# Order of the first chunks in a spectral-mixing + SwiGLU kernel: narrow rows from PSUM, split second layer, SyncE's queue reordered

## Chip, cores, metric

The kernel runs on one core of a Trainium2 chip. The metric is device time in microseconds (us) of one launch. A core has TensorE (PE, matrix products into PSUM), VectorE (DVE), ScalarE (ACT), GpSimd (POOL) and SyncE (SP), which here only issues DMAs. Each engine works through its own instructions in the order in which the program gives them, and waits where an operand isn't there or where a buffer is still in use. SP's and POOL's DMA issues are such instructions too: one that waits holds up everything behind it in its queue.

## What is computed

The input x is 4096 x 640 in fp32. The block is a layer norm with scale and shift from a condition vector (`h = LN(x)*(1+ca)+sa`), a Fourier mixer, a gated residual, a second modulated layer norm, a SwiGLU and a second gated residual:

```python
Xf = rfft2(h);  z = Xf.reshape(..., NB=4, BS=160)          # 4 blocks of 160 columns
hr = relu(zr@w1[0] - zi@w1[1] + b1[0]);  hi = relu(zi@w1[0] + zr@w1[1] + b1[1])     # layer 1
or_ = hr@w2[0] - hi@w2[1] + b2[0];       oi_ = hi@w2[0] + hr@w2[1] + b2[1]          # layer 2
Yf = softshrink(or_ + 1j*oi_, 0.01);     x = x + ga * irfft2(Yf)
x = x + gb * ((silu(h2@w_gate) * (h2@w_up)) @ w_down)      # h2: second modulated layer norm of x
```

Products are made to fp32 accuracy from a rounded upper part and a lower part (fp32r) of each factor: upper x upper, lower x upper, upper x lower. So each weight and each activation has an "upper" instruction (round) and a "lower" one (value minus upper).

## The kernel before

The transform over 4096 positions is split as 128 x 32. **Stage a** (dft_a, dft_c) transforms the eight tiles xa0 to xa7 (each 128 x 4 x 640) over the first index and writes them to DRAM with write_s1(t, f): f = 0 and f = 1 are a quarter of the rows each (320 KB per tile), f = 2 is the other half (640 KB per tile). The rows written with f = 0 feed chunks 0 and 1, those with f = 1 chunks 2 and 3, those with f = 2 chunks 4 to 7. load_g(ch) reads a chunk back in the other layout into g (1,280 KB, two buffers), so chunk 2 needs every f = 1 write landed, and chunk 2's buffer is chunk 0's.

**Per chunk** (eight chunks, blocks b = 0 to 3 of 160 columns = 128 wide + 32 narrow):
- stage_b(ch, t) (matmuls of L612): second transform of 128 columns into a PSUM bank pb; t = 0 to 3 are the wide columns of the blocks, t = 4 the four blocks' narrow 32 columns together. Its banks are single buffers "b0" (t < 4) and "b1" (t = 4); (0,1) and (0,3) use the pair "p2" instead.
- evac_b (L619 on ACT, L620 on DVE): upper and lower part of the wide columns, z.
- the narrow rows rz, all four blocks of which layer 1 needs as 128 partitions. For chunk 0, evac_r(0, b) makes them from PSUM, 2 ACT instructions (L642) and 2 DVE instructions (L652) of 32 partitions for each block. For chunks 1 to 7, rem_high (L662) and rem_low (L666) evacuate all of pb into rt, rem_move (L675) writes rt to DRAM, and rem_read (L681) reads it back in four DMAs with the partitions regrouped. For chunk 1 both go by POOL's queue, for the others by SP's.
- stage_l1(ch, b) (21 matmuls of L707): two 128-wide outputs in the PSUM pair "p1" and a third, narrow one in "p3"; ACT rounds with relu (L724, L725), DVE makes the lower part (L726); tail_l1 (L743, L744) the narrow rest r2.
- stage_l2(ch, b) (16 matmuls of L764, two groups q of eight, in the PSUM pair "p2"); DVE adds the bias b2t and writes tt (L766).
- later: move_x (L780, SP: tt regrouped into xx), shrink, the inverse transform stage_i and a write to s2 by POOL.

The loop over p = 4 ch + b (L879) interleaves these over chunks: at p it does stage_l1(p), the next chunk's stage_b, stage_l2(p - 1). For p = 0 (L885 to L895) all four stage_l1 of chunk 0 come first, then the six lower parts of layer 2's weights (weights_low, L286, on DVE); p = 1 to 3 then do stage_b(1, ...) and stage_l2(0, 0 to 2); p = 4 starts with stage_l1(1, 0).

**Weights of layer 2**: six jobs prep2 in the order w2a, w2a, w2b, w2b, w2c, w2c; each an upper part (weights_high, L281 on POOL) and a lower part (weights_low, L286 on DVE), 128 x 640.

**Memory that is reused.** The pool p2 (right side) takes over the memory of xa0 to xa7 tile by tile, each tile waiting only for the users of what lay there. Both pools end at the same edge; per partition xp has 8 x 10,240 = 81,920 bytes and p2 78,336, so p2 begins 3,584 bytes further in. Its tiles lie in the order of first use: acc, cl, wx, bx (6,656 bytes), w2a, w2b, w2c (10,240 each), tt (2 x 5,120), wm, xx, xh, xl, co.

**SP's queue** (L489 to L547): half of chunk 0's load, the weights w2 (L252, L253), write_s1 of tiles 2 and 3, load_g(1) (L310), b2t (L514), a 16-element copy s1h out of g1 (L515), so that SP waits there until g1 has landed, then write_s1 of tiles 0, 4, 5, 6, 7 for f = 1 and again for f = 2, load_g(2), small constants (idn, tx, bx) and the first of the mod_load (L547).

Of the kernel before, what the change touches and what calls it, by code (L numbers as in the profile page):

```python
# [171 lines left out]
def body(tc, x, w1, b1, w2, b2, wg, wu, wd, c, wm, k_fa, k_tb, k_tx, k_bm, k_bx, k_ga, k_ge, k_id, out, dbg=None):  # L172
# [10 lines left out]
    s2 = nc.dram_tensor("s2", (128, N2, D), F32, kind="Internal").ap()  # L183
    s1h = nc.dram_tensor("s1h", (1, 16), F32, kind="Internal").ap()
    rzd = nc.dram_tensor("rzd", (NCH, 128, 4, 258), F32, kind="Internal").ap()
# [16 lines left out]
    with ExitStack() as top:  # L202
# [34 lines left out]
        with ExitStack() as af:  # L237
# [95 lines left out]
            with tc.tile_pool(name="sp", bufs=1) as sp:  # L333
# [157 lines left out]
                for job in jobs[6:]:  # L491
                    weights_high(*job)
                write_s1(7, 0, rest)
                load_g(0, 16, 32, None, rest)
                raws[2] = load_weights(rp, w2, "2")
                for t in (2, 3):
                    for f in (1, 2):
                        write_s1(t, f)

# [9 lines left out]

            hp = af.enter_context(tc.tile_pool(name="hp", bufs=1, reuse_waits="tile"))  # L510
            load_g(1)
            load_tb(1)
            b2t = hp.tile([P, 2, NB, BS], F32, name="b2t")
            nc.sync.dma_start(b2t, b2.rearrange("r b o -> (r b o)").partition_broadcast(P))  # L514
            nc.sync.dma_start(s1h, gs[1][127:128, 3, 0:16])  # L515
            for f in (1, 2):
                for t in (0, 4, 5, 6, 7):
                    write_s1(t, f)
            load_g(2)
            load_tb(2)  # L520
            stx.close()

# [12 lines left out]
            prep2 = [prep2[k] for k in (0, 3, 1, 4, 2, 5)]  # L535
            for job in prep2:
                weights_high(*job, pool)
# [68 lines left out]
            def stage_b(ch, t):  # L606
                g, tb = gs[ch], tbs[ch]
                pb = (ps.tile([P, 2, 256], F32, tag="p2", name=f"pb{ch}_{t}") if (ch, t) in ((0, 1), (0, 3)) else
                      bank0(1 if t == 4 else 0, [P, 2, 256], f"pb{ch}_{t}"))
                col = slice(128 * t, 128 * t + 128)  # L610
                for j in range(4):
                    mm(pb[:, :, 64 * j:64 * j + 64], g[:, j, col], tb[:, j, :], start=True, stop=True)  # L612
                pbs[ch, t] = pb
# [59 lines left out]
            def rem_move(ch):  # L673
                NN = width(ch)
                (pool if ch == 1 else nc.sync).dma_start(rzd[ch, :, :, 0:NN], f32(rts[ch].rearrange("p l i k -> p (l i) k")[:, :, 0:NN]))  # L675

            def rem_read(ch):
                NN = width(ch)
                r = rzs[ch] = hp.tile([P, NB, 258], F32R, tag="rz", bufs=2, name=f"rz{ch}")
                for q in range(4):  # L680
                    (pool if ch == 1 else nc.sync).dma_start(f32(r[32 * q:32 * q + 32, :, 0:NN]),  # L681
                                      rzd[ch].rearrange("(b e) q k -> q e b k", b=NB)[q, :, :, 0:NN])

            def stage_l1(ch, b):
                NN = width(ch)
                z = zs[ch, b]
                r = rzs[ch][:, b, :]
                hs = []
                pls, seqs = [], []
                for o in range(2):  # L690
                    pls.append(ps.tile([P, 512], F32, tag="p1", name=f"pl{ch}_{b}_{o}"))
                    cs = slice(128 * o, 128 * o + 128)
                    cl = slice(256 + 128 * o, 384 + 128 * o)
                    seqs.append([(w1a[:, b, cs], z[:, 0, 0, :NN]), (w1a[:, b, cs], z[:, 1, 0, :NN]),
                                 (w1a[:, b, cl], z[:, 0, 0, :NN]),
                                 (w1b[:, b, cs], z[:, 0, 1, :NN]), (w1b[:, b, cs], z[:, 1, 1, :NN]),
                                 (w1b[:, b, cl], z[:, 0, 1, :NN]),
                                 (w1c[:, b, cs], r[:, :NN]), (w1c[:, b, cl], r[:, :NN])])
# [20 lines left out]
                for o in range(2):  # L719
# [5 lines left out]
                    act.activation(h[:, 0, :NN], pl[:, :NN], AF.Relu, bias=b1m[:, o, b:b + 1])  # L725
                    dve.tensor_tensor(h[:, 1, :NN], h32[:, :NN], f32(h[:, 0, :NN]), op=OP.subtract)  # L726
                    hs.append(h)
                if not early:
# [6 lines left out]
                act.activation(u0[:, :NN], pl[64:128, :NN], AF.Copy)  # L735
                dve.scalar_tensor_tensor(u1[:, :NN], pl[0:64, :NN], b1r[:, b:b + 1], u0[:, :NN],
                                         op0=OP.add, op1=OP.add)
                hss[ch, b] = (hs[0], hs[1], r2, u1)
# [9 lines left out]
            def stage_l2(ch, b, then=()):  # L748
                h0, h1, r2, _ = hss[ch, b]
                de = slice(160 * b, 160 * b + 160)  # L750
                for q in range(3 if ch == CE else 2):
# [3 lines left out]
                    if b == 0 and q < 2:  # L755
# [5 lines left out]
                           (h1[:, 0, fs], w2b[:, b, 320:320 + W]),  # L761
                           (r2[:, fs], w2c[:, b, 0:W]), (r2[:, fs], w2c[:, b, 320:320 + W])]
                    for i, (l, m) in enumerate(seq):
                        mm(pc[:M, :W], l, m, start=(i == 0), stop=(i == len(seq) - 1))  # L764
                    if q < 2:
                        dve.tensor_tensor(tts[ch, q][:, :, de], pc[:, :320].rearrange("p (r e) -> p r e", r=2),  # L766
                                          b2t[:, :, b, :], op=OP.add)
                        if then:
                            then[q]()
                    else:  # L770

                        dve.tensor_tensor(tts[ch, 0][0:1, 1, de], pc[0:1, :160], b2t[0:1, 0, b, :], op=OP.add)

            xxs = {}
# [102 lines left out]
            cf = []  # L877

            for p in range(LAST + 1):  # L879
                ch, b = p // 4, p % 4  # L880
                on(shrink, p - 6)
                if p > 3:
                    on(stage_l1, p)

                if p == 0:  # L885
                    for q in range(4):
                        stage_l1(0, q)
                        for t in ((1, 2), (3,), (), ())[q]:
                            stage_b(0, t)
                            evac_b(0, t)  # L890
                            evac_r(0, t)
                        tail_l1(0, q)
                    for job in prep2:
                        weights_low(*job)
                    continue  # L895
                elif b == 0:
                    todo = [(ch, 3)]
# [3 lines left out]
                for q in todo:  # L901
                    stage_b(*q)
                    if q[1] < 4:
                        evac_b(*q)
                for f, *a in sums.get(p, ()):
                    f(*a)
                if b == 1 and ch + 1 < NCH:
                    rem_high(ch + 1)
                if p > 3:
                    on(tail_l1, p)  # L910
                on(shrink_high, p - 6)
# [1567 lines left out]
```

## Time and profile before

| | us |
|---|---|
| median of 3 runs (lowest, highest) | 1466.19 (1465.18, 1467.83) |
| profiled execution: device time | 1462.63 |
| profiled execution: span, first to last instruction | 1460.8 |
| TensorE busy in the span | 1408.0 (96%) |
| mean granted TensorE clock | 0.994 |

The profile is of one execution. In it an instruction's row gives its start, its duration, the engine, the line, output <- inputs and, in brackets, how long the engine sat idle before it and what released it. "SPq" is an issue by SP. A row of the windows gives, for each engine, busy time and number of instructions, then the granted TensorE clock (1.00 is full), the busy share of the DMA engines and what they moved.

### The profile page before, as it was taken

How to read it: one execution, taken by the hardware profiler on the slowest of the kernel's cores; microseconds unless marked ns; L12 is line 12 of the kernel's file. 1: busy time of each engine (PE TensorE's matmuls, PEld its weight loads, DVE VectorE, ACT ScalarE, POOL GpSimd, SP SyncE). 2: the span in 40 equal slices, each digit the busy share in tenths (PEclk: the TensorE clock that was granted, in tenths of full speed). 3: DMA queues.
4: the chain of work that ended last, by engine and by line, in shares of the span. 5: the costliest groups of instructions: out<-in, count | busy, mean ns of one | idle time of the engine just before them, and what ended most of it. 6: DMA issues, size and time to landing. Idle time of an engine off the chain costs nothing.

```text
span 1460.8 us, 23921 instructions
## 1 busy us (share of the span) xinstructions
PE 1408.0 (96%) x8516; PEld 1331.2 (91%) x8516; DVE 1081.5 (74%) x1967; ACT 782.2 (54%) x1550; POOL 551.3 (38%) x647
## 2 busy tenths in 40 slices
PE   6969999998999999999999999999999999999998
PEld 2669999966888888899999999999999999999998
DVE  8848877878787797757787868787747767567775
ACT  7828888744545455544565546555435445245432
POOL 5300100044555354322445424444324545146533
PEclk9989999999999999999999999999999999999999
DMA  9877767748677998798977997877696666966552
GB/s 378 313 230 225 241 190 228 221 144 271 240 276 261 334 310 267 272 370 290 311 263 244 343 368 256 312 247 253 229 344 219 228 209 239 357 207 238 204 183 88
DMA packets 186473, 380.05 MB, mean 260 GB/s; under 512 B 22226, under 2 KB 104082, under 8 KB 184562
## 3 DMA queue, kind: packets, MB, share of 16 engines
q1 hardware_dynamic: 177826, 361.09, 71.9%
q0 software_dynamic: 6944, 14.82, 3.3%
q10 hardware_dynamic: 1584, 2.62, 0.5%
q8 instruction: 67, 1.10, 0.3%
q14 instruction: 52, 0.43, 0.1%
HBM read 263.91 MB, written 105.39 MB: 253 GB/s over the span
## 4 chain that ended last, share of the span: by engine, by line
PE 59%; DVE 8%; DMA 6%; issue 2%; ACT 2%; POOL 1%; SPq 0%; POOLq 0%; ACTq 0%; DVEq 0%
PE pd L2347 12%; PE pw L2026 7%; PE pw L2028 7%; PE pw L2027 7%; PE pd_X L2207 4%; DMA cr<-s 3%; PE pg L1890 2%; PE pg L1891 2%; PE pd_Y L2207 2%; PE pg L1892 2%; PE pw L2037 2%; PE pw L2038 2%; PE pw L2039 2%; DVE wb L1344 2%; PE pd_Z L2207 1%
## 5 line engine op out<-in xcount | busy, mean ns | idle before, releaser
L2347 PE MATMUL pd<-wdh,a 128*128 128x320 f32 x1040 | 238.9, 310 | 1.0 <-DVE a L1927 0.6
L2347 PEld LDWEIGHTS pd<-wdh,a 128*128 128x128 f32 x1040 | 176.2, 188 | 2.0 <-DVE a L1927 0.9
L1344 DVE TENSOR_TENSOR wb<-r,wb 128x512 fp32r<-128x512 f32 (+3 forms) x156 | 159.5, 1030 | 17.2 <-ACT wb L1341 14.6
L2347 PE MATMUL pd<-wdl,a 128*128 128x320 f32 x540 | 166.2, 309 | 0.0
L2026 PE MATMUL pw<-h,wt 128*128 128x384 f32 x416 | 140.9, 339 | 2.3 <-ACT s_x L2045 1.2
L2028 PE MATMUL pw<-h,wt 128*128 128x384 f32 x416 | 140.4, 337 | 0.0
L2027 PE MATMUL pw<-h,wt 128*128 128x384 f32 x416 | 139.8, 336 | 0.0
L1341 ACT ACTIVATE wb<-r 128x512 fp32r<-128x512 f32 (+3 forms) x172 | 117.9, 703 | 34.0 <-PE pw L2039 24.6
L2319 DVE TENSOR_TENSOR x<-x,pd 128x320 f32<-128x320 f32 x240 | 108.9, 477 | 36.4 <-PE pd L2347 32.6
L2028 PE MATMUL pw<-h,wb 128*128 128x384 f32 x312 | 105.1, 337 | 2.3 <-DVE wb L1344 2.3
L2026 PE MATMUL pw<-h,wb 128*128 128x384 f32 x312 | 105.4, 338 | 0.0
L2027 PE MATMUL pw<-h,wb 128*128 128x384 f32 x312 | 105.0, 336 | 0.0
L1890 PE MATMUL pg<-ht,wb 128*128 128x512 f32 x260 | 103.0, 396 | 1.5 <-ACT wb L1341 1.5
L1892 PE MATMUL pg<-ht,wb 128*128 128x512 f32 x260 | 101.7, 391 | 2.2 <-DVE wb L1344 2.2
L2347 PEld LDWEIGHTS pd<-wdl,a 128*128 128x128 f32 x540 | 101.4, 188 | 0.5
L1891 PE MATMUL pg<-ht,wb 128*128 128x512 f32 x260 | 101.4, 390 | 0.0
L2045 ACT ACTIVATE s_x<-pw 128x384 f32<-128x384 f32 x52 | 25.5, 490 | 114.3 <-PE pw L2028 113.6
L1603 POOL TENSOR_TENSOR cr<-cr,gab 128x640 f32<-128x640 f32 x28 | 47.4, 1694 | 103.2 <-DMA cr<-s 83.2
L2026 PEld LDWEIGHTS pw<-h,wt 128*128 128x128 f32 x416 | 78.3, 188 | 4.2 <-ACT s_x L2045 2.2
L821 POOL DMA_DIRECT2D s<-co x28 | 15.8, 564 | 168.2 <-ACT co L820 160.5
L2027 PEld LDWEIGHTS pw<-h,wt 128*128 128x128 f32 x416 | 78.3, 188 | 0.0
L2028 PEld LDWEIGHTS pw<-h,wt 128*128 128x128 f32 x416 | 78.3, 188 | 0.0
(335 smaller groups left out, 4054.3 us busy)
## 6 DMA issues: line engine op xcount, KB each, us to landing
wt<-td SPq DMA_DIRECT2D x104, 512.0 KB, 5.3
hs<-ho SPq DMA_DIRECT2D x52, 512.0 KB, 5.0
h<-hs SPq DMA_DIRECT2D x32, 768.0 KB, 8.4
r<-in_B_w_gate_dram SPq DMA_DIRECT2D x36, 640.0 KB, 4.9
r<-in_B_w_up_dram SPq DMA_DIRECT2D x36, 640.0 KB, 5.3
wdr<-wdd SPq DMA_DIRECT2D x21, 640.0 KB, 4.9
td<-wt SPq DMA_DIRECT2D x25, 512.0 KB, 5.4
g<-s SPq DMA_DIRECT2D x7, 1280.0 KB, 9.3
```

Of the source, the lines that this page charges most:

```text
L1341: act.activation(wbs[t, n][:, 0, ks, e], raw[t, n][:, ks, e], AF.Copy)
L1344: (pool if onp else dve).tensor_tensor(wbs[t, n][:, 1, ks, e], raw[t, n][:, ks, e], f32(wbs[t, n][:, 0, ks, e]), op=OP.subtract)
L1603: pool.tensor_tensor(crs[r], crs[r], gab, op=OP.mult)
L1890: mm(b, wh, hh, start=(kk == 0), stop=False)
L1891: mm(b, wh, hl, start=False, stop=False)
L1892: mm(b, wl, hh, start=False, stop=(kk == 4))
L2026: mm(b, w(0, kp), a[:, kp, 0], start=start and kp == 0, stop=False, skip_group_check=not start)
L2027: mm(b, w(0, kp), a[:, kp, 1], start=False, stop=False, skip_group_check=not start)
L2028: mm(b, w(1, kp), a[:, kp, 0], start=False, stop=kp == 1, skip_group_check=not start)
L2207: mm(bk[b, i][:, :320], x, y, start=new and j == 0, stop=j == len(seq) - 1, skip_group_check=not new)
L2319: dve.tensor_tensor(x2[:, e], x2[:, e], x[0][:, :320], op=OP.add)
L2347: mm(pd[g, hf][0][:, :320], l, m, start=i == 0, stop=i == len(s) - 1 and not (last and len(gs) > 1))
```

## The change

Four things are done. (1) Chunk 1's narrow rows are made from PSUM by evac_r, as chunk 0's are, and its rem_high, rem_low, rem_move and rem_read fall away. (2) The first blocks get an order of their own, first_blocks(): layer 2's lower parts come earlier (two after stage_l1(0, 1), four before stage_l1(0, 2)), the two upper parts of w2c go from POOL to ACT, stage_l1(0, 2)'s three DVE instructions are put off, stage_l2(0, 0) and (0, 1) come before stage_l1(0, 3), and stage_l2(0, 0) does all products that need no lower weight first, for both q, and the three others of each at the end. (3) stage_b(0, 3) uses "b0" instead of "p2". (4) On SP, the f = 1 writes of tiles 2 and 3 come ahead of chunk 0's last load, tile 4's writes and b2t ahead of load_g(1), the copy s1h is gone, and load_g(2) comes ahead of the f = 2 writes of tiles 6, 7 and 0.

```diff
                 write_s1(7, 0, rest)
+                for t in (2, 3):
+                    write_s1(t, 1)
                 load_g(0, 16, 32, None, rest)
                 raws[2] = load_weights(rp, w2, "2")
-                for t in (2, 3):
-                    for f in (1, 2):
-                        write_s1(t, f)
+                for t, f in ((2, 2), (3, 2), (4, 1), (4, 2)):
+                    write_s1(t, f)
...
+            b2t = hp.tile([P, 2, NB, BS], F32, name="b2t")
+            nc.sync.dma_start(b2t, b2.rearrange("r b o -> (r b o)").partition_broadcast(P))
             load_g(1)
             load_tb(1)
-            b2t = hp.tile([P, 2, NB, BS], F32, name="b2t")
-            nc.sync.dma_start(b2t, b2.rearrange("r b o -> (r b o)").partition_broadcast(P))
-            nc.sync.dma_start(s1h, gs[1][127:128, 3, 0:16])
-            for f in (1, 2):
-                for t in (0, 4, 5, 6, 7):
-                    write_s1(t, f)
+            for t in (5, 0, 6, 7):
+                write_s1(t, 1)
+            write_s1(5, 2)
             load_g(2)
             load_tb(2)
+            for t in (6, 7, 0):
+                write_s1(t, 2)
             stx.close()
...
-            for job in prep2:
+            for job in prep2[:4]:
                 weights_high(*job, pool)
...
-                pb = (ps.tile(..., tag="p2", ...) if (ch, t) in ((0, 1), (0, 3)) else
+                pb = (ps.tile(..., tag="p2", ...) if (ch, t) == (0, 1) else
                       bank0(1 if t == 4 else 0, [P, 2, 256], f"pb{ch}_{t}"))
...
-            def stage_l1(ch, b):
+            def stage_l1(ch, b, later=None):
...
-                    dve.tensor_tensor(h[:, 1, :NN], h32[:, :NN], f32(h[:, 0, :NN]), op=OP.subtract)
+                    lows.append(lambda h=h, h32=h32: dve.tensor_tensor(h[:, 1, :NN], ..., op=OP.subtract))
+                    if later is None:
+                        lows.pop()()
...
+                    if (ch, b) == (0, 0):
+                        late.append((pc, [seq[k] for k in (2, 5, 7)]))
+                        for i, k in enumerate((0, 1, 3, 4, 6)):
+                            mm(pc[:M, :W], *seq[k], start=(i == 0), stop=False)
+                        continue
...
+                for q, (pc, seq) in enumerate(late):
+                    for i, (l, m) in enumerate(seq):
+                        mm(pc[:, :320], l, m, start=False, stop=(i == 2))
+                    dve.tensor_tensor(tts[ch, q][:, :, de], pc[:, :320]..., b2t[:, :, b, :], op=OP.add)
...
+            def first_blocks():
+                stage_l1(0, 0)
+                for t in (1, 2):
+                    stage_b(0, t)
+                    evac_b(0, t)
+                    evac_r(0, t)
+                tail_l1(0, 0)
+                stage_l1(0, 1)
+                for job in prep2[:2]:
+                    weights_low(*job)
+                tail_l1(0, 1)
+                for job in prep2[4:]:
+                    weights_high(*job)
+                for job in prep2[2:]:
+                    weights_low(*job)
+                later = []
+                stage_l1(0, 2, later)
+                stage_b(0, 3)
+                stage_l2(0, 0)
+                evac_b(0, 3)
+                evac_rh(0, 3)
+                stage_l2(0, 1, (lambda: evac_rl(0, 3), lambda: None))
+                for f in later:
+                    f()
+                stage_l1(0, 3)
+                tail_l1(0, 2)
+                for t in (4, 0):
+                    stage_b(1, t)
+                evac_b(1, 0)
+                tail_l1(0, 3)
+                evac_r(1, 0)
+                stage_l2(0, 2)
+                stage_b(1, 1)
+                evac_b(1, 1)
+                evac_r(1, 1)
+                stage_b(1, 2)
+                evac_b(1, 2)
...
             for p in range(LAST + 1):
+                if p == 0:
+                    first_blocks()
+                if p < 4:
+                    for f, *a in mods.get(p, ()):
+                        f(*a)
+                    continue
...
+                if p == 4:
+                    evac_r(1, 2)
+                    evac_r(1, 3)
```

## What was predicted before the run

> **What bounds the kernel now.** I read the page's busy shares first, then who TensorE waited for, then its timeline where those waits lie, then the windows.
>
> ```profile
> PE 1408.0 (96%) x8516; PEld 1331.2 (91%) x8516; DVE 1081.5 (74%) x1967; ACT 782.2 (54%) x1550; POOL 551.3 (38%) x647
> ```
> ```profile
> PE pl L707 <- DMA rz<-rzd: 7.8, 1, 7.8
> ```
> ```profile
> 60.00:100.00 40.00, 26.40 (x170) 24.80 (x170) 21.64 (x39) 15.04 (x34) 14.08 (x14) 0.83 0.89 313
> 100.00:200.00 100.00, 100.00 (x781) 99.62 (x780) 76.90 (x145) 82.09 (x168) 9.75 (x28) 1.00 0.71 212
> ```
>
> TensorE is idle for 1460.8 - 1408.0 = 52.8 us in all, and one long wait lies where the change works: 7.8 us for chunk 1's narrow rows coming back from DRAM. From 60 to 100 us TensorE is busy for 26.4 of 40, from 100 to 200 for all of 100. So what reaches 100 us earlier finds no slack that could swallow it: a microsecond won before 100 us is one at the end, as long as DMAs follow. The timeline of that stretch:
>
> ```profile
> 63.64 1.05 PE L612 MATMUL pb<-tb,g 128*128 128x128 f32 x8
> ...
> 68.11 0.62 PE L707 MATMUL pl<-z,w1a 128*128 128x256 f32 x3 [0.90 <-ACT h L725]
> ...
> 75.72 0.41 PE L764 MATMUL pc<-w2a,h 128*128 128x320 f32 x1 [2.74 <-DVE w2a L286]
> ...
> 77.18 0.63 PE L764 MATMUL pc<-w2b,h 128*128 128x320 f32 x1 [0.71 <-DVE w2b L286]
> ...
> 78.72 0.64 PE L764 MATMUL pc<-w2c,r 128*128 128x320 f32 x1 [0.63 <-DVE w2c L286]
> ...
> 97.28 0.77 PE L707 MATMUL pl<-rz,w1c 128*128 128x256 f32 x2 [7.79 <-DMA rz<-rzd]
> ...
> 100.42 1.05 PE L612 MATMUL pb<-tb,g 128*128 128x128 f32 x8
> 101.22 0.69 PE L764 MATMUL pc<-w2a,h 128*128 128x320 f32 x3
> ...
> 103.65 0.52 PE L707 MATMUL pl<-z,w1a 128*128 128x256 f32 x3
> ...
> 106.17 1.95 PE L612 MATMUL pb<-tb,g 128*128 128x128 f32 x16
> ```
>
> From the starts of the last four rows, undisturbed: one stage_b takes 101.22 - 100.42 = 0.80 us of TensorE, one stage_l2 2.43, one stage_l1 2.52. From the end of stage_l1(0,1) at 63.64 to the start of stage_l1(1,1) at 103.65 the program does 3 stage_l1, 6 stage_b and 4 stage_l2: 7.56 + 4.80 + 9.72 = 22.1 us of work in 40.0 us. So **17.9 us are lost**. The gaps in brackets give 0.90 + 2.74 + 0.71 + 0.63 + 7.79 = 12.8; the other 5.1 is a slower clock:
>
> ```profile
> 75.00:80.00 5.00, 2.94 (x10) 2.23 (x11) 4.98 (x7) 0.00 (x0) 0.00 (x0) 0.63 1.04 417
> 80.00:85.00 5.00, 5.00 (x28) 5.00 (x28) 2.03 (x4) 0.69 (x1) 0.77 (x1) 0.69 0.96 340
> 85.00:90.00 5.00, 4.49 (x34) 4.28 (x32) 2.22 (x5) 0.69 (x1) 2.25 (x4) 1.00 1.00 283
> ...
> 95.00:100.00 5.00, 2.72 (x13) 2.75 (x14) 0.43 (x1) 0.99 (x3) 0.00 (x0) 0.50 0.12 31
> ```
>
> The column behind POOL's is the granted clock, then come the DMA engines' busy share and GB/s: the clock is 0.63 and 0.69 after the first group of gaps, 0.50 after the long one.
>
> **The change part by part.** The same matmuls remain between those two points, so the new length is 22.1 us plus the waits that the new order brings. I walk it in the new order.
>
> ```profile
> 63.45 0.47 ACT L725 ACTIVATE h<-pl,b1m 128x256 fp32r<-128x256 f32 x1
> ```
> ```profile
> 65.14 0.48 DVE L736 SCALAR_TENSOR_TENSOR u<-pl,b1r,u 64x256 f32<-64x256 f32 x1
> ...
> 73.65 0.42 DVE L744 SCALAR_TENSOR_TENSOR r<-u,r 64x256 fp32r<-64x256 f32 x1 [0.48 <-ACT r L743]
> 74.10 1.56 DVE L286 SCALAR_TENSOR_TENSOR w2a<-rm,w2a 128x640 fp32r<-128x640 f32 x2
> 75.58 1.55 DVE L286 SCALAR_TENSOR_TENSOR w2b<-rm,w2b 128x640 fp32r<-128x640 f32 x2
> 77.05 0.88 DVE L286 SCALAR_TENSOR_TENSOR w2c<-rr,sgn,w2c 128x640 fp32r<-128x640 f32 x1
> 77.84 0.82 DVE L286 SCALAR_TENSOR_TENSOR w2c<-rr,w2c 128x640 fp32r<-128x640 f32 x1
> ```
>
> *stage_l1(0,2)* follows stage_l1(0,1) directly and needs a "p1" bank that ACT is still reading; the first is free when ACT's second reading ends, 63.45 + 0.47 = 63.9: wait 0.3. ACT then does r2 and the two uppers of w2c. The trace has no upper of this shape on ACT; I price one at 0.8 us, near DVE's row of the same 128x640 (bounds: 0.68, ACT's 128x512 in row L662 below, and 0.88, the dearest w2c row). Both are done at about 67.7, and stage_l2(0,0) wants them at about 68. Hidden.
>
> *Layer 2's lower parts.* DVE is through with stage_l1(0,1) at 65.6. Behind it stand w2a (1.56), r2 (0.42), w2b (1.55), w2c (0.88 + 0.82), together 5.2, less some 0.3 of overlap: ready at about 70.6, against 78.7 before. Putting stage_l1(0,2)'s three DVE instructions off is what keeps this queue short. TensorE reaches the last lower product at 63.64 + 0.3 + 2.52 + 0.80 + 12 x 0.15 = 69.1 (0.15 is 2.43 / 16): **wait 1.6** (bounds 1.3 and 1.8, with twice that overlap and with none) in place of 2.74 + 0.71 + 0.63. Then stage_l2(0,1) needs the "p2" bank that DVE's first bias add frees: 0.3.
>
> *stage_l1(0,3)* then needs stage_b(0,3)'s parts (ACT and DVE finish them during stage_l2(0,1)): no wait. The late three instructions of DVE come before its first evacuation, about 74 us, just in time.
>
> *Narrow rows of chunk 1.* Each evac_r costs 2 ACT and 2 DVE instructions:
>
> ```profile
> L652 DVE SCALAR_TENSOR_TENSOR rz<-pb,ca,rz 32x256 fp32r<-32x256 f32 x6 | 2.9, 485 | 0.7 <-ACT rz L642 0.7
> L642 ACT ACTIVATE rz<-pb,ca 32x256 fp32r<-32x256 f32 x6 | 2.8, 470 | 0.4 <-DVE rz L652 0.3
> ...
> L666 DVE SCALAR_TENSOR_TENSOR rt<-pb,ca,rt 128x512 fp32r<-128x512 f32 x1 | 0.7, 740 | 0.0
> L662 ACT ACTIVATE rt<-pb,ca 128x512 fp32r<-128x512 f32 x1 | 0.7, 682 | 0.0
> ```
>
> Eight of each: 3.8 us of ACT for 0.7, 3.9 us of DVE for 0.7. DVE was busy 21.6 of the 40 us from 60 to 100, so about 3 us more lies beside TensorE. The whole way through DRAM goes, and with it the 7.79. What is late next is "b0", now with nothing between stage_b(1,1) and (1,2): TensorE waits from the end of the one for ACT's 0.69 and DVE's 0.75, with their starts **1.75 us**, against hidden before.
>
> Sum: 0.3 + 1.6 + 0.3 + 1.75 = 3.95 us of new waits, so 26.0 us instead of 40.0, and stage_l1(1,1) starts at about 89.6 instead of 103.65: **14.0 us**. The clock should hold through gaps of 1.6 and 1.75 us some 10 us apart: it dropped after three gaps that come to 4.1 us within 6, and again within the 7.79.
>
> *SP's queue* decides whether data are there.
>
> ```profile
> 57.62 2.05 PE L612 MATMUL pb<-tb,g 128*128 128x128 f32 x16 [0.36 <-DMA g<-s]
> ```
> ```profile
> 52.00:54.00 2.00, 2.00 (x17) 1.93 (x17) 1.20 (x5) 0.69 (x1) 0.00 (x0) 1.00 0.28 102
> 54.00:56.00 2.00, 1.60 (x12) 1.40 (x13) 1.53 (x3) 0.93 (x2) 0.00 (x0) 1.00 0.58 164
> ...
> 60.00:62.00 2.00, 1.17 (x8) 0.92 (x8) 1.73 (x4) 1.64 (x4) 2.00 (x2) 1.00 1.01 428
> ```
> ```profile
> 68.58 0.31 SPq L515 DMA_DIRECT2D s1h<-g  x1
> ...
> 86.78 0.43 SPq L541 DMA_DIRECT2D bx<-in_k_bx_dram  x1
> 87.25 0.83 SPq L547 DMA_DIRECT2D wm<-in_w_mod_dram  x1
> 103.98 5.02 SPq L780 DMA_DIRECT2D xx<-tt  x8
> ```
>
> The two writes (640 KB) put ahead of chunk 0's last load cost TensorE between 0 (they fit into the stretch where the DMA engines were 0.28 to 0.58 busy) and 1.5 us (640 KB at 428 GB/s, all in front), since stage_b(0,1) waits for that load. I take 0.5, nearer the idle rows.
>
> ```profile
> g<-s SPq DMA_DIRECT2D x7, 1280.0 KB, 9.3
> ```
>
> g1 landed at 68.58, where SP went on; now 960 KB more lie ahead (tile 4's 960 and b2t's 640, less the 640 moved forward): 2.3 us, so 71; it is wanted at about 76.5. b2t and tile 4's writes go out right behind the earlier ones and should have landed by 68; the first bias add wants both at 71. load_g(2) must wait for the f = 1 writes: 1,280 KB and tb1's 256 behind g1, 3.7 us at 428 GB/s, so about 75 to 76; at 9.3 us to landing (the last row) it is there at 85, and stage_b(2,4) wants it at 92. On SP the constant bx, whose memory is xa0's, now waits for the last write, (0,2). The DMA engines ran empty at about 95.6 (0.12 of the last window above); 1.5 MB fewer lie ahead (1 MB of rzd both ways, 0.5 MB of constants and wm), at the 283 GB/s of 85 to 90 us 5.3 us: (0,2) lands at about 90. move_x stands behind it, and is wanted at 90, with some 1.5 us until ACT needs its data. Cost nothing, if barely.
>
> Total 14.0 - 0.5 = **13.5 us**. On the profiled execution's own time that is 1462.63 - 13.5 = 1449.1; the median of the runs shown stands 3.56 above that execution, and on it I forecast 1466.19 - 13.5 = **1452.7 us**.
>
> **Rivals.** *The clock drops in the new gaps.* The two dips in the windows cost 5 x 0.37 + 5 x 0.31 = 3.4 us for the first. For it: the first dip followed gaps of which none was over 2.74, and mine are 1.6 and 1.75. Against: dense work lies between them. It gives 1452.7 + 3.4 = 1456. [...]
>
> *SP is late.* If (0,2) lands 4 to 6 us after 90, bx, wm and move_x slip, then ACT, which reads xx in order ahead of layer 1's evacuation: 1455 to 1457.
>
> *Slower: DVE stands still on a reused tile.*
>
> ```profile
> 80.34 0.49 DVE L766 TENSOR_TENSOR tt<-pc,b2t 128x320 f32<-128x320 f32 x1 [0.36 <-DMA s<-xa]
> ```
>
> The first bias add did wait for a write of xa, because tt lies where an xa lay. By the sizes, tt begins 3,584 + 6,656 + 30,720 = 40,960 bytes in, which is xa4, written early now. Were it a tile whose f = 2 write has become last, the add at 71 would stand until 89, DVE behind it, TensorE too with both "p2" banks held: 18 us and a slow clock of some 3, so 1452.7 + 21 = 1474. It decides from a landing after about 85. Only the arithmetic speaks against it, and the row can't tell tile 0 from tile 4.
>
> *It does not reach the end.* A later stage that waits for something not moved, say DMAs (0.71 busy from 100 to 200), would take it back: 1466. The full TensorE rows speak against it.
>
> **How the numbers follow.** Forecast 0.70, clock 0.10, SP 0.09, standstill 0.06, taken back 0.05. Runs scatter by some 1.5 us and the unknown costs by about 3, so the range is 1448.5 to 1460: it holds the forecast, the clock and SP, and leaves out the last two. A measurement tells about 0.2% (2.9 us) from no change: faster 0.89, same 0.05, slower 0.06.
>
> **What would show it.** Right: no wait for rzd, lower weights ready near 70.6, gaps of 1 to 2 us at the last lower products of stage_l2(0,0) and before stage_b(1,2), clock 1.00 from 60 to 105, stage_l1(1,1) starting near 90, the same spacing after that. Wrong: DVE idle at the first tt, TensorE waiting for g in chunks 1 or 2, ACT waiting for xx, or a gain at 90 us that is smaller at the end.

## The result and the profile after

| | us |
|---|---|
| before: median of 4 runs (lowest, highest) | 1466.22 (1465.18, 1467.83) |
| changed: median of 4 runs (lowest, highest) | 1454.73 (1453.17, 1457.64) |
| ratio, 95% interval | 0.9923 [0.9904, 0.9942] |
| forecast for the changed kernel | 1452.7 (1448.5 to 1460) |

The change takes 11.5 us off; 13.5 were forecast. Two later comparisons of the same kernel gave 0.9921 [0.9897, 0.9944] and 0.9927 [0.9910, 0.9944], 12.2 and 10.4 us by the medians, so the gain is 1 to 3 us smaller than forecast, and the question below is which step those 2 us belong to. The profiled execution of the changed kernel took 1457.64 us, the longest of its four, and that of before 1462.63, below its median; the two profiles therefore differ by 5 us only, and times are compared by medians, stages by the profiles. The profile of e3 is of an execution at a granted clock of 0.65 that took 2002.46 us, so e3 is read by its other 11 runs and by a second profile, e5.

The page of the changed kernel, busy times:

```profile
PE 1410.7 (97%) x8516; PEld 1331.4 (91%) x8516; DVE 1089.2 (75%) x1974; ACT 785.8 (54%) x1559; POOL 543.6 (37%) x640
```

TensorE has the same 8516 matmuls. ACT and DVE have a few more instructions (the narrow rows in slices of 32 partitions), POOL seven fewer. The two windows that were shown of before, now of the changed kernel (columns: length, then busy time and count of PE, PEld, DVE, ACT, POOL, then granted clock, DMA share, GB/s):

```profile
60.00:100.00 40.00, 35.56 (x255) 33.77 (x254) 30.51 (x59) 25.82 (x57) 8.23 (x7) 0.96 0.83 291
100.00:200.00 100.00, 99.75 (x778) 98.62 (x777) 78.82 (x150) 82.90 (x170) 10.26 (x29) 1.00 0.77 234
```

TensorE is busy 35.6 of the 40 us where it was busy 26.4, and 255 matmul records lie there instead of 170. The waits from 60 to 150 us, largest of TensorE:

```profile
PE pb L613 <- DVE z L621: 1.6, 1, 1.6
...
PE pc L788 <- DVE w2c L285: 1.1, 1, 1.1
```

The 7.8 us for chunk 1's rzd are gone. What is left are the two waits that the prediction named: the bank "b0" ahead of stage_b(1, 2), and the last lower part of w2c. TensorE's timeline through the stretch (start, duration, line, what, idle before):

```profile
64.16 0.29 PE L709 MATMUL pl<-rz,w1c 128*128 128x256 f32 x1
64.60 0.62 PE L709 MATMUL pl<-z,w1a 128*128 128x256 f32 x3 [0.15 <-ACT h L727]
...
68.02 0.55 PE L774 MATMUL pc<-w2a,h 128*128 128x320 f32 x2
...
70.32 0.41 PE L788 MATMUL pc<-w2b,h 128*128 128x320 f32 x1 [0.42 <-DVE w2b L285]
71.86 0.41 PE L788 MATMUL pc<-w2c,r 128*128 128x320 f32 x1 [1.12 <-DVE w2c L285]
...
72.40 0.30 PE L788 MATMUL pc<-w2c,r 128*128 128x320 f32 x1
72.86 1.17 PE L777 MATMUL pc<-w2a,h 128*128 128x320 f32 x3
...
76.82 0.52 PE L709 MATMUL pl<-z,w1a 128*128 128x256 f32 x3
...
83.45 1.05 PE L613 MATMUL pb<-tb,g 128*128 128x128 f32 x8
86.07 1.16 PE L613 MATMUL pb<-tb,g 128*128 128x128 f32 x8 [1.57 <-DVE z L621]
...
92.79 0.52 PE L709 MATMUL pl<-z,w1a 128*128 128x256 f32 x3
```

Stage_l1(0, 1) ends at 64.28 (0.12 behind the start of its last matmul, the spacing within a stage), and stage_l1(1, 1) starts at 92.79: **28.5 us**, against 40.0 before and 26.0 forecast. The same rows of a run of the unchanged file in a later comparison (e12 below):

```profile
63.57 0.29 PE L709 MATMUL pl<-rz,w1c 128*128 128x256 f32 x1
64.01 0.62 PE L709 MATMUL pl<-z,w1a 128*128 128x256 f32 x3 [0.15 <-ACT h L727]
...
67.43 0.55 PE L774 MATMUL pc<-w2a,h 128*128 128x320 f32 x2
...
71.35 0.30 PE L788 MATMUL pc<-w2c,r 128*128 128x320 f32 x1
71.79 0.71 PE L777 MATMUL pc<-w2a,h 128*128 128x320 f32 x3
...
74.25 0.52 PE L709 MATMUL pl<-z,w1a 128*128 128x256 f32 x3
...
80.92 1.05 PE L613 MATMUL pb<-tb,g 128*128 128x128 f32 x8
83.54 1.16 PE L613 MATMUL pb<-tb,g 128*128 128x128 f32 x8 [1.57 <-DVE z L621]
...
90.26 0.52 PE L709 MATMUL pl<-z,w1a 128*128 128x256 f32 x3
```

From 63.69 to 90.26 it is 26.6 us. The differences of starts, less the work that the prediction priced, give a ledger:

| wait or loss in the stretch, us | forecast | e12 | first profile |
|---|---|---|---|
| "p1" bank ahead of stage_l1(0, 2) | 0.3 | 0.32 | 0.32 |
| last lower products of stage_l2(0, 0) | 1.6 | 3.92 + 0.15 - 2.43 = 1.64 | 4.38 + 0.15 - 2.43 = 2.10 |
| "p2" bank ahead of stage_l2(0, 1) | 0.3 | 0.29 | 0.31 |
| stage_l2(0, 1) slower than its 2.43 | 0 | 2.46 - 2.43 = 0.03 | 3.96 - 2.43 = 1.53 |
| "b0" ahead of stage_b(1, 2) | 1.75 | 2.62 - 0.80 = 1.82 | 2.62 - 0.80 = 1.82 |
| the rest: work, priced at 22.1 | 22.1 | 22.5 | 22.4 |
| sum | 26.0 | 26.6 | 28.5 |

Each of the four waits came out within 0.1 us of its price where the clock held. In the first profile stage_l2(0, 1) ran for the most part at a granted clock of 0.50 (72.80 to 76.22), 3.96 us for 2.43, and the wait for the lower parts was 0.5 us longer.

### The profile page after: what moved, and what is told of

The parts are those of the page before. It is cut to its first block, busy times and chain, and to the rows that moved or that the text cites. A ratio compares the mean times of both kernels' runs of the same rounds, so it can differ in the third digit from the quotient of the medians.

```text
span 1455.9 us, 23927 instructions
## 1 busy us (share of the span) xinstructions
PE 1410.7 (97%) x8516; PEld 1331.4 (91%) x8516; DVE 1089.2 (75%) x1974; ACT 785.8 (54%) x1559; POOL 543.6 (37%) x640
## 3 DMA queue, kind: packets, MB, share of 16 engines
q10 hardware_dynamic: 1584, 2.62, 0.5%
## 4 chain that ended last, share of the span: by engine, by line
PE 75%; DVE 10%; DMA 7%; ACT 3%; issue 2%; POOL 2%; SPq 1%; DVEq 0%; ACTq 0%; POOLq 0%
PE pd L2399 13%; PE pw L2078 8%; PE pw L2080 8%; PE pw L2079 7%; PE pc L777 4%; PE pd_X L2259 4%; PE pl L709 4%; PE pg L1942 2%; PE pg L1943 2%; PE pg L1944 2%; PE pd_Y L2259 2%; PE pw L2089 2%; PE pw L2091 2%; PE pw L2090 2%; DMA cr<-s 2%
```

## Experiments

All times of a group are set against runs of the kernel before on the same chip: medians 1467.35 (e1 to e4), 1466.27 (e5 to e8) and 1465.67 (e9 to e12).

### e1 and e12: the changed kernel again

No edit; e12 was run beside e9 to e11.

> The changed kernel again, unedited. Theory A (the gain is made between stage_l1(0,1) and stage_l1(1,1) and only blurred later): 11 to 12 us faster than before in the median; in this profile the stretch from the end of stage_l1(0,1) to the start of stage_l1(1,1) takes 27 to 28.5 us of TensorE against 40.0 before, 1.7 us less where no half-clock window falls on layer 2; what is lost between 260 and 400 us (6 us in the first profile) differs from run to run, by the half-clock windows that happen to fall there. Theory B (a later stage takes part of the gain back, each time): the loss of about 5 us between 250 us and the end is there again, with the same waits.

> The changed kernel, for the comparison with the rows alone: 11 to 12.5 us faster than before, 1.5 to 3 us faster than the rows alone (rival: within 1 us).

Measured: e1 1455.16 us (1451.5 to 1458.05), e12 1455.27 (1452.0 to 1458.68), both ratios above. All 16 runs of this kernel have their median at 1455.2. In neither profile does the clock drop between 60 and 300 us (the first half-clock stretches begin at 316.8 and 343.4); the stretch takes 27.0 us in e1 and 26.6 in e12. Whether a later stage takes part of the gain back (theory B) is taken up below, under the rivals.

### e2 and e11: only the narrow rows

Before, with chunk 1's rows made from PSUM, each block's right behind its evac_b; e11 is the same file again.

```diff
                     if q[1] < 4:
                         evac_b(*q)
+                        if q[0] == 1:
+                            evac_r(*q)
...
-                if b == 1 and ch + 1 < NCH:
+                if b == 1 and 0 < ch < NCH - 1:
                     rem_high(ch + 1)
...
```

> The kernel before, with chunk 1's narrow rows made from PSUM and nothing else of the change. Theory A: the 7.79 us wait for rzd goes and so does the half clock after it (1.5 to 2 us on stage_l1(1,0)), less up to 1 us of extra work on DVE between the first bias adds: 8 to 9 us faster than before, 1457 to 1458. The gaps of 2.74, 0.71 and 0.63 for layer 2's lower weights stay. Rival (the DMA queue, which ran full until 95 us, is the bound and another load is waited for in place of rzd): g of chunk 2 becomes the wait, 3 to 5 us faster at most.

> The narrow rows alone once more, beside the changed kernel on one chip. Theory A (gains at 150 us carry to the end): the rows alone were 8.1 us ahead of before at 150 us in their profile, the changed kernel 9.8 with and 11.3 without a half-clock window, so the rows alone are 1.5 to 3 us slower than the changed kernel in the median. Rival (the other three parts of the change are worth nothing, as the first medians with 11.2 and 12.2 us would allow): within 1 us of each other.

Measured: 1456.14 us, ratio 0.9931 [0.9910, 0.9952], and 1458.19, ratio 0.9934 [0.9917, 0.9951]. By the ratios that is about 10 us of 1467, most of the whole gain, from this part alone, with the old order on SP. In its group e11's median lies 2.9 us above that of the changed kernel (e12), as expected; e2's lies 1.0 above e1's. TensorE's rows of e2, starts of stage_l1(1, 1) and of stage_l1(2, 0):

```profile
95.07 0.52 PE L707 MATMUL pl<-z,w1a 128*128 128x256 f32 x3
...
114.05 0.52 PE L707 MATMUL pl<-z,w1a 128*128 128x256 f32 x3
```

Stage_l1(1, 1) starts 103.65 - 95.07 = 8.6 us earlier than before. From there to stage_l1(2, 0) it takes 114.05 - 95.07 = 18.98 us; that number returns below.

### e3 and e5: all but the narrow rows

The changed kernel, with chunk 1's rows sent through DRAM by POOL's queue, as before; e5 is the same file again.

```diff
-                nc.sync.dma_start(rzd[ch, ...], ...)
+                (pool if ch == 1 else nc.sync).dma_start(rzd[ch, ...], ...)
...
                 evac_b(1, 0)
+                rem_high(1)
                 tail_l1(0, 3)
-                evac_r(1, 0)
+                rem_low(1)
+                rem_move(1)
+                rem_read(1)
...
```

> The changed kernel, but chunk 1's narrow rows take the way through DRAM on POOL's queue as before. Theory A: their lower part is ready at about 83.5 us, the write lands 6 to 7 us later, the four reads another 8 to 10 us, so they are back at 96 to 99 us as before, whatever else is earlier; stage_l1(1,0) gets there at 86 and waits 8 to 11 us at a falling clock: only 1 to 3 us faster than before, 1463 to 1465. Rival (the parts simply add): the rows cost the 9 us that their wait and clock cost before and the other parts keep theirs, 2.5 to 3 us faster by 11.5 - 8.7, or 5 to 7 us faster if the wait stays 7.8 and all before it moves up.

> The changed kernel with chunk 1's narrow rows by way of DRAM, a second time, for an undisturbed profile. It was 0.2% slower than before (-0.0 to +0.3%), where I expected 1 to 3 us faster. Theory A' (the rows' way back depends on DMA issues and on a DMA queue that is full until 90 us, so it ends when it ended before, at 97 us, or later, since the first lower part comes from DVE behind more work): a wait for rz<-rzd of 9 to 12 us before stage_l1(1,0), that ends at 96 to 99 us, with a half-clock stretch behind it. Rival (the loss comes later than 100 us): the wait is 6 us or less, and time is lost after it.

Measured: e3 1468.09 us (the median of the 11 runs), ratio 1.0016 [0.9999, 1.0033]; e5, one run, 1462.77, which lies among the runs of before beside it (1461.70 to 1468.75). The gain of 1 to 3 us expected of e3 isn't there, and the adding of the parts, its rival, isn't either. Why, is in e5's rows, first TensorE's, then POOL's:

```profile
97.97 0.77 PE L709 MATMUL pl<-rz,w1c 128*128 128x256 f32 x2 [12.19 <-DMA rz<-rzd]
```
```profile
82.52 0.77 POOL L676 DMA_DIRECT2D rzd<-rt  x1 [13.61 <-DVE tt L779]
91.89 2.24 POOL L682 DMA_DIRECT2D rz<-rzd  x4 [8.59 <-DMA rzd<-rt]
```

The rows are wanted earlier, but their way through DRAM ends where it ended before: at 97.97 instead of 97.28. The write goes out at 82.52, against 80.29 before, and POOL stands 8.6 us from the end of its issue until it can issue the read (the write landed after 8.0 of them); TensorE goes on 97.97 - 94.13 = 3.8 us behind the end of the read's issue. TensorE waits 12.2 us where it waited 7.8. So the earlier order of layer 2 is all given back in that one wait: **the parts of the change don't add up**. The rows alone give about 10 us, the rest alone nothing that can be told from scatter, and the rest on top of the rows some 2 us (1455.2, the median of 16 runs, against 1457.4, that of the 12 of e2 and e11), little against runs of one kernel that lie 4 to 7 us apart.

### e4: the old order of SP's queue

The changed kernel with the copy s1h and every write_s1, load_g and b2t issue in their old places.

```diff
-                for t in (2, 3):
-                    write_s1(t, 1)
                 load_g(0, 16, 32, None, rest)
                 raws[2] = load_weights(rp, w2, "2")
-                for t, f in ((2, 2), (3, 2), (4, 1), (4, 2)):
-                    write_s1(t, f)
+                for t in (2, 3):
+                    for f in (1, 2):
+                        write_s1(t, f)
...
+            nc.sync.dma_start(s1h, gs[1][127:128, 3, 0:16])
+            for f in (1, 2):
+                for t in (0, 4, 5, 6, 7):
+                    write_s1(t, f)
             load_g(2)
...
```

> The changed kernel with the old order of SP's queue, the copy s1h that makes SP wait for chunk 1 included. Theory A (the order on SP is needed, because tt lies where xa4 lay): stage_l2(0,0)'s first bias add on DVE waits for tile 4's last write, which lands at about 80 to 81 us as before instead of before 71; DVE and, with both banks of p2 held, TensorE stand 8 to 9 us, then half clock: 1 to 4 us faster than before only, 1462 to 1465. Rival (SP's order is of no account, the compute order does it all): within 1 us of the changed kernel.

Measured: 1465.61 us, ratio 0.9992 [0.9975, 1.0008]: the gain is gone. DVE's row and TensorE's:

```profile
81.05 0.89 DVE L788 TENSOR_TENSOR tt<-pc,b2t 128x320 f32<-128x320 f32 x2 [9.37 <-DMA s<-xa]
```
```profile
81.60 1.17 PE L776 MATMUL pc<-w2a,h 128*128 128x320 f32 x3 [8.97 <-DVE tt L788]
```

DVE's first bias add stands 9.4 us for a write of an xa, and TensorE stands 9.0 us behind it, since both "p2" banks are held; stage_l2(0, 1) then takes 4.43 us instead of 2.43, at a granted clock of 0.50 (72.42 to 86.07). This is the standstill that the prediction had as its rival for the slower side, with half its price. It does not strike the changed kernel because of its order on SP. The trace tells which write it is, too: the add is released at 80.86, by the landing of the write that SP issued at 76.62, and by SP's order (f = 1 for tiles 0, 4, 5, 6, 7, then f = 2 for the same) that is tile 4's for f = 2. In the profile of before it is the same write, issued at 75.33 and landed at 80.15, ahead of the add at 80.34. So the prediction's arithmetic on tt and xa4 is borne out. The new order of the first blocks needs the SP part: without it its gain, and that of the rows with it, is lost in this wait. The rows alone don't need it (e2).

### e6: the rows of blocks 2 and 3 behind layer 2

evac_r(1, 2) and (1, 3) move behind stage_l2(0, 3), so that this stage's bias adds don't stand behind them on DVE.

```diff
                         evac_b(*q)
-                if p == 4:
-                    evac_r(1, 2)
-                    evac_r(1, 3)
...
                 on(stage_l2, p - 1)
+                if p == 4:
+                    evac_r(1, 2)
+                    evac_r(1, 3)
```

> The changed kernel with evac_r(1,2) and evac_r(1,3) moved behind stage_l2(0,3), so that its bias adds on DVE don't stand behind 2 us of narrow rows. Theory (in the changed kernel these adds end 3 us later against stage_l1(1,1) than before, so move_x, and behind it on SP rem_move of chunk 2, are late, and chunk 2's layer 1 waits 0.6 us for rz and more for xx): the 1.1 us that the changed kernel loses between stage_l1(1,1)'s start and 150 us shrink to 0.3 or less. Rival (it is the added DVE and ACT work itself, or SP's late constants): the 1.1 us stay, within 0.2.

Measured: 1454.85 us, one run. To see what this tells, the first profiles' starts of stage_l1(2, 0) are needed, before and then changed:

```profile
122.63 0.52 PE L707 MATMUL pl<-z,w1a 128*128 128x256 f32 x3
```
```profile
112.74 0.52 PE L709 MATMUL pl<-z,w1a 128*128 128x256 f32 x3
```

From stage_l1(1, 1) to stage_l1(2, 0) before takes 122.63 - 103.65 = 18.98 us, as e2 does; the changed kernel 112.74 - 92.79 = 19.95: **1.0 us is lost** behind the stretch, with the clock at 1.00. In the changed kernel DVE makes the rows of both blocks, and only then adds the bias of stage_l2(0, 3), 3 us behind the start of stage_l1(1, 1):

```profile
94.34 1.00 DVE L653 SCALAR_TENSOR_TENSOR rz<-pb,ca,rz 32x256 fp32r<-32x256 f32 x2 [1.02 <-ACT rz L643]
...
95.83 0.89 DVE L779 TENSOR_TENSOR tt<-pc,b2t 128x320 f32<-128x320 f32 x2
```

e6's rows on TensorE, stage_l1(1, 1), the stage_b behind it, stage_l1(1, 2) and stage_l1(2, 0):

```profile
91.05 0.52 PE L709 MATMUL pl<-z,w1a 128*128 128x256 f32 x3
...
94.83 1.38 PE L613 MATMUL pb<-tb,g 128*128 128x128 f32 x10 [1.11 <-DVE rz L653]
...
99.07 0.41 PE L709 MATMUL pl<-z,w1a 128*128 128x256 f32 x2
...
111.40 0.52 PE L709 MATMUL pl<-z,w1a 128*128 128x256 f32 x3
```

From stage_l1(1, 2) on, e6 runs as before did (111.40 - 99.07 = 12.33 us; before 122.63 - 110.31 = 12.32). In the changed kernel the same piece takes 112.74 - 99.63 = 13.11 us, so 0.8 of the lost microsecond lie here, and moving the rows behind the adds removes them. The way there is by tt: move_x, which empties tt, goes out at 96.34 in the changed kernel and at 92.86 in e6, and the next adds of the changed kernel stand for it:

```profile
101.28 0.49 DVE L779 TENSOR_TENSOR tt<-pc,b2t 128x320 f32<-128x320 f32 x1 [1.01 <-DMA xx<-tt]
104.05 0.49 DVE L779 TENSOR_TENSOR tt<-pc,b2t 128x320 f32<-128x320 f32 x1 [2.28 <-DMA xx<-tt]
```

So the rows that DVE makes ahead of the adds are the cause of most of the lost microsecond. But moved behind them they hold the bank "b1", whose narrow columns they read, and stage_b(2, 4) waits 1.1 us for that. In all e6 takes 111.40 - 91.05 = 20.35 us where the changed kernel takes 19.95: one wait for another, and 1.4 us more than before where at most 0.3 were expected. In e2, where each block's rows come singly behind its own stage_b, neither is lost. That order inside the changed kernel was not tried.

### e7, e8, e9: the remaining waits taken one by one

e7 puts stage_l1(1, 0) ahead of stage_b(1, 2) and stage_l2(0, 3) ahead of stage_b(1, 3), so that "b0" has time to come free. e8 also puts r2 of (0, 1) behind the lower parts on DVE. e9 also gives stage_b(2, 4) a bank of "p3" and makes the rows of blocks 2 and 3 later.

```diff
                 evac_r(1, 1)
+                stage_l1(1, 0)
                 stage_b(1, 2)
                 evac_b(1, 2)
+                tail_l1(1, 0)
+                stage_l2(0, 3)
+                stage_b(1, 3)
+                evac_b(1, 3)
+                evac_r(1, 2)
+                evac_r(1, 3)
...
```
```diff
-                tail_l1(0, 1)
                 for job in prep2[4:]:
                     weights_high(*job)
                 for job in prep2[2:]:
                     weights_low(*job)
+                tail_l1(0, 1)
```
```diff
+                      ps.tile([P, 2, 256], F32, tag="p3", ...) if (ch, t) == (2, 4) else
...
+                if p in (4, 5):
+                    evac_r(1, p - 2)
```

> The changed kernel with stage_l1(1,0) ahead of stage_b(1,2) and stage_l2(0,3) ahead of stage_b(1,3) and of evac_r(1,2) and (1,3), so that the single bank b0 has layer work between its two uses. Theory: the 1.57 us wait for DVE's z before stage_b(1,2) goes, and so do the 1.1 us lost after stage_l1(1,1): 2.5 to 3 us earlier at 150 us than the changed kernel in the same clock, 14 us ahead of before without a half-clock window and 12.5 with one. Rival (TensorE only waits elsewhere, for rz of block 1 or the banks of p2): 1 us or less.

> As the last one, and r2 of block (0,1) on DVE and ACT moved behind layer 2's lower weights, so that the last of them is ready 0.4 us earlier. Theory: the last lower product's wait shrinks from 1.12 to about 0.7 us; 13 us (with one half-clock window on layer 2) to 14.6 us (without) ahead of before at 150 us; in the median 14 to 16 us faster than before, 2 to 3 us faster than the changed kernel. Rival (what is won here is lost in the later stages, as 4 us were between 250 us and the end in both profiles of the changed kernel): median not below the changed kernel's by more than 1 us.

> The last order once more, with stage_b(2,4) in a bank of p3 instead of b1, and evac_r(1,2) and (1,3) one and two steps later, so that nothing waits for chunk 1's narrow rows to leave b1. Theory (b1, held until evac_r(1,3), is the bound that took the place of b0: TensorE waited 1.1 to 2.3 us for it in three kernels): no wait of stage_b(2,4) for DVE rz, no half-clock window at 94 us, 13.5 to 14.5 us ahead of before at 150 us, median 2 to 3 us below the changed kernel. Rival (DVE and ACT carry too much between 85 and 105 us, whatever the bank): another wait of 1 us or more takes its place, 11 to 12 us ahead at 150 us.

Measured: e7 1459.82 us in one run; e8 1454.10, ratio 0.9922 [0.9902, 0.9942]; e9 1454.09, ratio 0.9918 [0.9901, 0.9934]. TensorE of e7 at stage_b(2, 4), and then the waits of e9 from 60 to 150 us:

```profile
93.64 2.65 PE L613 MATMUL pb<-tb,g 128*128 128x128 f32 x16 [2.29 <-DVE rz L653]
```
```profile
DVE tt L780 <- DMA xx<-tt: 6.9, 4, 3.1
PE pc L778 <- DVE tt L780: 1.8, 2, 1.0
```

In e7 and e8 the 1.57 us for "b0" become 2.29 for "b1". In e9 neither is left, the wait for the last lower part is 0.8 us instead of 1.1, but DVE stands 6.9 us for the transfer that empties tt (3.2 in e12), and TensorE 1.8 us for DVE (0.2 in e12). Each removed wait was replaced, as the rivals had it: at stage_l1(2, 0) the three are 10.9, 11.1 and 11.8 us ahead of before, the changed kernel without the half clock 11.7 and 12.5 (e1, e12). None of the three beats the changed kernel by more than the scatter of its runs.

### e10: keeping TensorE busy in the wait

The changed kernel with six products of ones, into a bank that nothing reads, ahead of the last two lower products of the first group.

```diff
+                if late:
+                    pz = ps.tile([P, P], F32, tag="p1", name="pzl")
                 for q, (pc, seq) in enumerate(late):
                     for i, (l, m) in enumerate(seq):
+                        for _ in range((0, 2, 4)[i] * (q == 0)):
+                            mm(pz, ones, ones, start=True, stop=True)
```

> The changed kernel, with six products of ones (128 x 128, nothing reads them) put into TensorE's wait for the last lower weights: two ahead of the second lower product, four ahead of the third. Theory (the first profile's half clock from 72.80 to 76.22 came from the idle time in the 3.41 us ahead of it): no half-clock window between 65 and 80 us, 11.0 to 11.4 us ahead of before at 150 us, as the profiles without that window. Rival (the half clock has another cause): the window comes as often as before. Median 0 to 1 us below the changed kernel by the first, the same by the second.

Measured: 1455.24 us, ratio 0.9919 [0.9896, 0.9943], the same as the changed kernel. The fill does what it is for, by the window of 3.41 us that holds the wait:

```profile
68.50:71.91 3.41, 3.40 (x25) 3.05 (x24) 2.90 (x5) 2.93 (x7) 0.39 (x1) 1.00 1.02 364
```

TensorE is busy for all of it and the clock holds (1.00 in it and in the next one, 71.91 to 75.33). But the clock held in e1 and e12 without the fill too, so the run doesn't show that it saves anything on average.

## Why the prediction was right in direction and 2 us too good

**The stretch.** Right: 17.9 us lost, four new waits of 3.95 in their place. They measured 4.07 in e12 (0.32 + 1.64 + 0.29 + 1.82). The work priced at 22.1 was 22.5, 0.4 more. Of the 5.1 us that the working puts down to the slower clock before, my estimate from the trace is 4.2: in the windows at a clock of 0.50 (76.25 to 83.08 and 93.32 to 100.15) TensorE was busy for 5.48 and 2.87 us, and half of that is taken as lost. A stage_l2 that lies wholly at that clock, in e4, took 4.43 us for 2.43, 0.45 of its time lost; by that it would be 3.8. By the first count the first dip cost 2.7 us and not the 3.4 of the rival, which counts idle time in.

**Layer 2's lower parts.** Right in kind. The last row of them on DVE:

```profile
70.98 0.82 DVE L285 SCALAR_TENSOR_TENSOR w2c<-rr,w2c 128x640 fp32r<-128x640 f32 x1
```

They were ready at 71.8, forecast 70.6; about 0.65 us of that is stage_l1(0, 1), which ended that much later in this execution. The two uppers of w2c on ACT took 0.81 and 0.72 us, priced at 0.8, and TensorE didn't wait for them.

**SP's queue.** Right that it costs nothing; the 0.5 us held against chunk 0's load weren't needed. TensorE's row at that load, then SP's issues:

```profile
58.07 2.05 PE L613 MATMUL pb<-tb,g 128*128 128x128 f32 x16 [0.17 <-DMA g<-s]
```
```profile
58.67 0.64 SPq L309 DMA_DIRECT2D g<-s  x1
...
73.43 0.49 SPq L350 DMA_DIRECT2D s<-xa  x1
...
91.39 0.33 SPq L542 DMA_DIRECT2D bx<-in_k_bx_dram  x1
...
96.34 5.02 SPq L798 DMA_DIRECT2D xx<-tt  x8
```

The wait for g was 0.17 us, against 0.36 before. g1 is in at about 73.4, where the next issue goes on (forecast 71, wanted 76.5). bx goes out at 91.4 (forecast: its cover lands at about 90). move_x goes out at 96.34, later than the 90 at which it was wanted, but not for SP: it follows the bias adds of 95.83.

**The first failed step: "about 3 us more lies beside TensorE".** The evac_r work does lie beside matmuls, but on DVE it stands ahead of stage_l2(0, 3)'s bias adds, and so it is paid for later, 1.0 us between stage_l1(1, 1) and stage_l1(2, 0) (20.0 in e1 and 19.9 in e12, against 18.98). e6 shows the cause of 0.8 of it, and e2 that it isn't a price of the rows but of their place. I had counted instructions and not what is queued behind them.

**The second: "the clock should hold through gaps of 1.6 and 1.75 us".** It held in e1 and e12 and fell in the first profile, where it cost 1.5 us, not the 3.4 of the rival. The windows that begin and end with the half-clock stretch of 72.80 to 76.22, in the changed kernel:

```profile
69.39:72.80 3.41, 1.78 (x9) 1.04 (x7) 2.90 (x6) 2.77 (x7) 0.00 (x0) 1.00 1.05 386
72.80:76.22 3.42, 3.36 (x12) 3.37 (x13) 1.91 (x5) 0.00 (x0) 0.00 (x0) 0.50 1.06 392
```

TensorE was busy for 1.78 of 3.41 us, and for the next 3.41 us the granted clock was 0.50. In e1 the window edges, found in the same way from its later half-clock stretches, lie elsewhere and cut the same gaps in two:

```profile
67.63:71.04 3.41, 2.33 (x15) 1.85 (x13) 3.35 (x6) 3.31 (x8) 0.30 (x1) 1.00 0.99 335
71.04:74.45 3.41, 2.80 (x17) 2.54 (x18) 2.47 (x5) 0.85 (x2) 0.00 (x0) 1.00 1.09 396
```

With 2.33 and 2.80 busy the clock stays at 1.00. With the gap ahead of stage_b(1, 2) wholly in one window of the first profile, the clock of the next stayed at 1.00:

```profile
83.04:86.46 3.42, 1.85 (x15) 1.66 (x15) 2.94 (x7) 1.71 (x4) 0.00 (x0) 1.00 0.98 313
86.46:89.87 3.41, 3.41 (x31) 3.41 (x31) 1.91 (x4) 2.17 (x5) 0.00 (x0) 1.00 1.10 420
```

So the second failed step is one of some runs, not of every run: the gaps at the last lower products come to 1.63 of 3.41 us in the first profile, where they lie in one window and the next had 0.50; in e1 an edge at 71.04 falls into the second of them, and the clock of both windows and of the next was 1.00. That the place of the edges decides is my reading of these two profiles, and it isn't all: after the window from 83.04, with 3.42 - 1.85 = 1.57 us idle, the clock was 1.00.

**The sum.** From the 13.5 forecast, in us: 0.5 more for the load that cost nothing, 0.6 less for the stretch (26.6 against 26.0), 1.0 less behind it: 12.4 where the clock holds. In the first profile 28.5 - 26.6 = 1.9 less again, 1.5 of it the clock: 10.5. At the start of stage_l1(2, 0) the three profiles of this kernel (the first, e1, e12) are in fact 9.9, 11.7 and 12.5 us ahead of before, 11.3 in the mean; the first has the 0.65 us of its later first blocks in it. The medians of the three comparisons lie 11.5, 12.2 and 10.4 below before, 11.4 in the mean. So the stretch, the microsecond behind it and, in one of these three profiles, a half clock account for the missing 2 us within the scatter of the medians. How often the clock falls at this place wasn't counted beyond that, so its share stays open.

**The rivals.** "The clock drops" happened in part of the runs. "SP is late" didn't. "DVE stands still" happened in e4, for 9.4 us, and not in the changed kernel, with its order of the queue. "Taken back later" is shown for 1 us, and for all in e3 and e5, the parts without the rows. Beyond that it stays open: against the profile of before, the leads of 9.9, 11.7 and 12.5 us at stage_l1(2, 0) have become 4.9, 7.2 and 10.6 at the end of the span. But that profile is of an execution 3.6 us under its median, and e4, which has no gain to lose, falls back against it too, from 0.8 us ahead to 2.6 behind, while e5 does not, from 1.0 behind to 0.2. The medians, as far apart as the early leads, ask for no later loss; since only one execution of before was profiled, a small one is not ruled out.

## What to carry to other kernels

Find the wait that ends last in a stage and ask of each part of a change whether it moves that end: the faster order ahead of a transfer whose end did not move was given back in full (e5: 12.2 us of wait for 7.8), and the fix of the transfer alone was most of the gain (e2: about 10 us). When work moves from a DMA to an engine that has time, look at what stands behind it in that engine's queue, and at the buffer that it holds (0.8 us in e6, a wait of 2.29 in e7), not at the engine's busy share. Before a new order is tried, work out for each reused buffer which transfer it waits for, and put that transfer early: in this order, without it, the whole gain was lost (e4: 1465.61 us).

## What the runs showed of the hardware beyond that

**In these profiles half clock came in stretches of 3.41 us or a multiple of it, each after 3.41 us in which TensorE was idle for 1.5 us or more.** From 40 to 690 us of each of 12 profiles (the first two and e1, e2, e4, e5 and e7 to e12; in e6 the mean clock of the whole execution is 1.0) the granted clock in these stretches is 0.50, and the stretches lie on one grid of 3.41 us, at another place in each execution (an edge at 72.80 in the first profile, at 71.04 in e1). I laid that grid over the 650 us of each and took the windows at full clock in which TensorE was busy under 2.3 us. After all 27 with at most 1.6 us busy the next window had half the clock. After the 18 between 1.66 and 1.91 it had so 5 times. After the 35 from 1.95 up to 2.3 it never had. The idle time need not be one long gap: in the first profile 3.41 - 1.78 = 1.63 us in several pieces, of 0.42 and 1.12 us and some tenths, was followed by half clock. These are counts of one kernel and its variants; what sets the clock, and why the 18 went both ways, they don't show.
